# Row maxima of a softmax attention: negated in the reduction, transposed in 32x32 squares on VectorE, and brought to the query rows over DRAM instead of by a TensorE transpose

## The chip, the cores and the metric

The kernel runs on one core of a Trainium2 chip. The metric is the device time of one execution in microseconds; the median of three runs of the kernel before is 1742.61 us (1740.09 to 1744.63).

## The reference

One transformer block with adaptive layer norm, for 2048 rows of 512 numbers, all in float32:

```
mod = silu(c) @ w_mod                            # six rows of 512: sa, ca, ga, sb, cb, gb
h = layernorm(x) * (1 + ca) + sa
q, k, v = split(h @ wqkv)                        # 32 heads of 16
p = softmax(q @ k.T / 4)                         # 2048 x 2048 per head
x = x + ga * ((p @ v) @ wo)
h = layernorm(x) * (1 + cb) + sb
x = x + gb * (mish(h @ w1 + b1) @ w2)            # 1792 hidden columns
```

The softmax is a stable one: the largest score of each query row is taken off before the exponential. This document is about the way of these maxima.

## The kernel before, in words

Every float32 product is made of rounded pieces: a number is split into a high part (type float32r) and the low rest, and three products (high by high, high by low, low by high) are added in PSUM.

**Attention.** The work is cut into 32 groups of four heads by one block of 512 queries (`NIT`; group n = 8 * block + heads). A group has 16 steps. In a step of group n TensorE makes four score products of that group (`score`, L505: 128 keys by 512 queries, each with a contraction of 64 rows), four products of a later group for its maxima (`max_tile`, L468: 128 queries by 512 keys), eight products of probabilities by values for the step two before (`pv`, L523), and up to eight half products of other work (L130, through `mm_half`): projections of q, k and v for later blocks, then the output projection and the feed-forward part of an earlier block. ScalarE turns each score bank into probabilities (L508). VectorE reduces each bank of L468 to one column of maxima (L470, tile `mx`).

**The maxima, before.** The maxima run `PRO` = 20 steps ahead of the scores: those of group n are complete at the end of step 16n - 5. `neg_max` (L474) then makes the maximum over the four key blocks, twice, into the two halves of `mm` (L479). `max_rows` (L483) is called at the end of the next step through the table `ats`: TensorE transposes `mm` into a bank of the ring (L485), so that 128 queries by 32 columns become 32 rows; VectorE writes `mh` = -max rounded to float32r (L487), and `mt` (L488), which holds on the high rows -max rounded and on the low rows the rest, by a column `lows` of zeros and minus ones that is made at the start (L75 to L78). Four DMAs then write `mt` into rows 48 and 49 (and 112 and 113) of the query tiles `qa` of the group's two pairs of heads (L494). The key tiles hold ones in these rows, so the score product itself takes the maximum off. The first scores of the group read them in step 16n, four steps after `max_rows`.

**What sets the order.** Everything is written out by one loop over steps (`step`, L1091). A step has two half steps, and work that isn't a product is put in a table `hooks` by half step with `at` (L183): loads, puts and short VectorE work. Engines run their own instructions in that order and wait on semaphores. All DMAs are issued by SyncE, in the order of the hooks, on one queue; a DMA whose data or place isn't ready holds SyncE and all DMAs behind it. Others that the text speaks of: `load_q` and `load_k` (L291, L300) bring query and key rows from DRAM; `qk_unit`'s `put` (L250, L254) writes projected queries and keys to DRAM from the tiles `qh` and `ql`, which ScalarE fills from PSUM (L240); `prep_unit` (L645 to L657) splits weights and puts them to DRAM (`w1scr`, `woscr`, `w2scr`), in groups 1 to 7; `load_split` (L662) brings them back for the feed-forward part from group 8 on; `evac` (L531 on) sends the row sums as `rc` to DRAM (L559) and reads them back spread over rows (`rb`, L561).

**PSUM.** Six banks form a ring (`ring`, L145) for L468, L505, the transpose of L485 and some short products; two more (`ms`, `acc`) take the other work and the sums of L523.

Of the kernel before, what the change touches and what calls it, by code (L numbers as in the profile page):

```python
# [8 lines left out]
F32 = mybir.dt.float32  # L9
F32R = mybir.dt.float32r  # L10
AF = mybir.ActivationFunctionType
ALU = mybir.AluOpType
AX = mybir.AxisListType
# [5 lines left out]
def adaln_block(ctx: ExitStack, tc: tile.TileContext, x, wqkv, wo, w1, b1, w2, c, w_mod, out):  # L19
    nc = tc.nc  # L20
    P = 128
# [6 lines left out]
    TB = 512  # L28
# [3 lines left out]
    NIT = NB * G  # L32
# [6 lines left out]
    PRO = 16 + LEAD  # L39
# [7 lines left out]
    out = out[0]  # L47
# [3 lines left out]
    cst = ctx.enter_context(tc.tile_pool(name="cst", bufs=1))  # L51
    dram = ctx.enter_context(tc.tile_pool(name="dram", bufs=1, space=DRAM))
# [6 lines left out]
    w1scr = dram.tile([FT, P, 2, D], F32, name="w1scr")  # L59
    w2scr = dram.tile([FT, P, 2, D], F32, name="w2scr")  # L60
    rscr = dram.tile([NIT, 4, TB], F32, name="rscr")

    ident = cst.tile([P, P], F32, name="ident")
    make_identity(nc, ident)
# [7 lines left out]
    nc.gpsimd.memset(sel, 0.0)  # L72
    for k in range(DK):
        nc.gpsimd.memset(sel[32 * k:32 * k + 1, :], 1.0)
    lows = cst.tile([P, 1], F32, name="lows")  # L75
    nc.vector.tensor_reduce(out=lows[:32], in_=ident[:32, :32].rearrange("p (a v q) -> p v a q", a=4, v=2)[:, 1], op=ALU.add,
                            axis=AX.XY)
    nc.vector.tensor_scalar_mul(lows[:32], lows[:32], -1.0)  # L78
    modc = cst.tile([P, 4, DK], F32, name="modc")
    sil = cst.tile([P, DK], F32, name="sil")  # L80
    b1c = cst.tile([P, FT], F32, name="b1c")
# [2 lines left out]
    def dap(t, off, ap):  # L84
        return bass.AP(tensor=t.tensor, offset=t.offset + off, ap=ap)
# [59 lines left out]
    def ring(w=1):  # L145
        if w == 2 and ring_at[0] % 2:
            ring_at[0] += 1
        b = ring_at[0] % NRING
        ring_at[0] += w
        return ring_t[:, b, :] if w == 1 else ring_t[:, b:b + 2, :]  # L150
# [32 lines left out]
    def at(h, f):  # L183

        hooks.setdefault(h, []).append(f)


    NR = 5
    kq = ctx.enter_context(tc.tile_pool(name="kq", bufs=1))
    ka = [kq.tile([P, S], F32R, name=f"ka{i}") for i in range(2)]  # L190
    qa = [kq.tile([P, TB], F32R, name=f"qa{i}") for i in range(NR)]
# [257 lines left out]
    ap = ctx.enter_context(tc.tile_pool(name="ap", bufs=1, reuse_waits="tile"))  # L449
# [24 lines left out]
    def neg_max(n):  # L474

        mx = mxs.pop(n)
        mm = ap.tile([P, 4, 2, 4], F32, tag="mm", name="mm", bufs=2)
        for v in range(2):
            nc.vector.tensor_reduce(out=mm[:, :, v, :], in_=mx.rearrange("p s (j q) k -> p (s j) q k", j=2), op=ALU.max,  # L479
                                    axis=AX.X)  # L480
        ats.setdefault(16 * n + 16 - PRO, []).append(lambda: max_rows(n, mm))

    def max_rows(n, mm):  # L483
        pt = ring()
        nc.tensor.transpose(pt[:32, :P], mm.rearrange("p a v q -> p (a v q)"), ident)  # L485
        mh, mt = [ap.tile([32, P], F32R, tag=t, name=t, bufs=1) for t in ("mh", "mt")]
        nc.vector.tensor_scalar_mul(mh, pt[:32, :P], -1.0)  # L487
        nc.vector.scalar_tensor_tensor(mt, mh.bitcast(F32), lows[:32], pt[:32, :P], op0=ALU.mult, op1=ALU.subtract)  # L488

        def put():  # L490
            for j in range(2):
                for s in range(2):
                    o = (2 * s + j) * 8
                    nc.sync.dma_start(  # L494
                        qa[(2 * n + j) % NR][64 * s + 48:64 * s + 50, :].rearrange("v (s q) -> v s q", s=4).bitcast(F32),
                        mt[o:o + 8, :].bitcast(F32))
        at(2 * (16 * n + 16 - PRO) + 3, put)

    pts = {}

# [541 lines left out]
    ats = {}  # L1042
# [48 lines left out]
    def step(t):  # L1091
# [4 lines left out]
        if t < 0:  # L1096

            for i in range(2):
                if tm < 16:
                    kb, jq = divmod(2 * tm + i, 8)  # L1100
                else:
                    jq, kb = tm % 16 // 2, 2 * second + i
                for s in range(2):
                    max_tile(tm // 16, jq // 4, s, jq % 4, kb)()
            if second and tm % 16 == 15:
                neg_max(tm // 16)
            run_hooks(2 * t + 1)
            for f in ats.pop(t, []):
                f()
            whole_units(2 * t + 1, CREDIT)  # L1110
            do_specials(2 * t + 1)
            return
# [53 lines left out]
        if tm < T and tm % 16 == 15:  # L1166
            neg_max(tm // 16)
# [121 lines left out]
    t = T + 2  # L1289
# [32 lines left out]
```

## Time and profile before

| | |
|---|---|
| median of three runs | 1742.61 us (1740.09 to 1744.63) |
| the profiled execution | 1738.89 us, span 1737.1 us |
| TensorE busy | 1702.3 us (98%), 12396 instructions |
| VectorE busy | 1464.9 us (84%), 2464 |
| ScalarE busy | 1349.4 us (78%), 2581 |
| GpSimd busy | 729.0 us (42%), 723 |
| SyncE's DMA queue | 237.92 MB, its packets 48.0% of 16 DMA engines' span |
| mean granted TensorE clock | 0.998 |

How to read the profile: the page gives shares of the span for each engine (PE = TensorE matmuls, PEld = its weight loads, DVE = VectorE, ACT = ScalarE, POOL = GpSimd, SP = SyncE), the chain of work that ended last, and groups of instructions by line of the kernel. A row of a timeline is: start in us from the span's start, duration in us, engine, line, operation, written tile <- read tiles, shapes, count of merged instructions, and in brackets the idle time of the engine just before it with what ended that wait. "SPq" are SyncE's issues of DMAs: their duration is that of the issue and not of the transfer. A row of a group is: line, engine, operation, tiles, shapes, count | busy us in total, mean ns of one | idle us before them and what ended it. A row of the waits is: who waited <- for whom: us in total, times, longest us. The durations of matmuls are modelled and overlap, so distances between starts tell more than they do.

### The profile page before, as it was taken

Reading aid. Unit: us, or ns where it says so; the run is one execution under the profiler, and the core shown is the slowest. Engines: PE = TensorE matmul, PEld = TensorE weight load, DVE = VectorE, ACT = ScalarE, POOL = GpSimd, SP = SyncE. Lnnn points to the kernel's source line nnn. Section 1 sums busy time; section 2 is a strip of 40 time slices with the busy share of each in tenths; the row PEclk is TensorE's granted clock in tenths of the full one; section 3 lists DMA queues with packets and bytes.
Section 4 is the critical chain, followed back from the end, with each engine's and each line's share of the span. In section 5 each row is a group of like instructions: output and inputs, shape, how many; then the busy total and the mean of one; then the engine's idle time right before and its main releaser. Section 6 shows DMA issues by size and latency. Waiting matters only on the chain.

```text
span 1737.1 us, 33698 instructions
## 1 busy us (share of the span) xinstructions
PE 1702.3 (98%) x12396; PEld 963.9 (55%) x12396; DVE 1464.9 (84%) x2464; ACT 1349.4 (78%) x2581; POOL 729.0 (42%) x723
## 2 busy tenths in 40 slices
PE   7999999999999999999999999999999999999999
PEld 5755655555435555555555555555555555554587
DVE  6987888888898998989889898888898999892377
ACT  6257777777777898888877898888878988888474
POOL 5131124665303373444523374434423464444552
PEclk9999999999999999999999999999999999999999
DMA  7777467777762432524353533434252543423261
GB/s 251 187 254 189 114 172 202 234 235 223 218 184 52 136 96 77 136 77 121 89 137 87 162 97 88 139 90 124 71 156 73 152 102 103 115 79 130 85 230 61
DMA packets 113997, 240.08 MB, mean 138 GB/s; under 512 B 24048, under 2 KB 49648, under 8 KB 107784
## 3 DMA queue, kind: packets, MB, share of 16 engines
q1 hardware_dynamic: 113832, 237.92, 48.0%
q8 instruction: 98, 1.61, 0.4%
q14 instruction: 67, 0.55, 0.1%
HBM read 179.95 MB, written 51.44 MB: 133 GB/s over the span
## 4 chain that ended last, share of the span: by engine, by line
PE 80%; DMA 8%; DVE 4%; POOL 2%; ACT 2%; issue 2%; SPq 1%; POOLq 0%; ACTq 0%; DVEq 0%
PE bk L523 26%; PE ring L468 19%; PE ring L505 18%; PE bk L130 12%; PE ring L124 2%; DMA qscr<-ql 2%; DVE mx L470 2%; PE ring L1028 1%; DMA w1scr<-hl 1%; ACT pr L508 1%; PE bk L124 1%; DMA woscr<-hl 1%; DMA xt<-in_A_x 1%; DMA kscr<-ql 1%; DMA hl<-in_B_w 1%
## 5 line engine op out<-in xcount | busy, mean ns | idle before, releaser
L470 DVE TENSOR_REDUCE mx<-ring 128x1 f32<-128x512 f32 x2048 | 1274.0, 682 | 166.5 <-PE ring L468 134.7
L508 ACT ACTIVATE pr<-ring 128x512 f32<-128x512 f32 x2048 | 1083.3, 603 | 256.1 <-PE bk L130 161.4
L468 PE MATMUL ring<-ka,qa 64*128 64x512 f32 x2048 | 850.6, 429 | 0.9 <-DVE mx L470 0.4
L505 PE MATMUL ring<-qa,ka 64*128 64x512 f32 x2048 | 726.1, 398 | 7.0 <-ACT pr L508 5.8
L468 PEld LDWEIGHTS ring<-ka,qa 64*128 64x128 f32 x2048 | 366.4, 184 | 414.2 <-DVE mx L470 334.5
L523 PE MATMUL bk<-pr,vg 128*32 128x512 f32 x4096 | 546.3, 606 | 0.0
L505 PEld LDWEIGHTS ring<-qa,ka 64*128 64x128 f32 x2048 | 374.1, 185 | 88.3 <-ACT pr L508 34.4
L130 PE MATMUL bk<-h,w 64*128 64x512 f32 (+1 forms) x1080 | 279.0, 392 | 1.4 <-ACT pr L508 1.3
L130 PE MATMUL bk<-w,a_h 64*128 64x512 f32 x608 | 204.9, 416 | 1.4 <-ACT pr L508 1.2
L130 PEld LDWEIGHTS bk<-h,w 64*128 64x128 f32 x1080 | 178.5, 184 | 19.0 <-ACT pr L508 8.7
L723 POOL TENSOR_TENSOR hb<-hb,ee 128x512 f32<-128x512 f32 x42 | 54.0, 1286 | 293.9 <-DVE ee L722 293.9
L523 PEld LDWEIGHTS bk<-pr,vg 128*32 128x32 f32 x4096 | 81.6, 108 | 131.8 <-issue 126.0
L130 PE MATMUL bk<-w,a_l 64*128 64x512 f32 x304 | 119.4, 393 | 0.0
L130 PEld LDWEIGHTS bk<-w,a_h 64*128 64x128 f32 x608 | 100.9, 184 | 10.4 <-ACT pr L508 5.8
L865 POOL TENSOR_TENSOR y<-yd,y 128x512 f32<-128x512 f32 x48 | 62.0, 1295 | 80.4 <-ACT yd L864 80.2
L736 POOL TENSOR_TENSOR qq<-ee,rr 128x512 f32<-128x512 f32 x42 | 54.3, 1292 | 76.9 <-ACT rr L729 76.7
L130 PE MATMUL bk<-w,o_hl 64*128 64x512 f32 x288 | 81.5, 414 | 2.2 <-POOL o_hl L93 1.1
L96 POOL TENSOR_TENSOR a_l<-hb,a_h 128x512 fp32r<-128x512 f32 x53 | 72.3, 1363 | 4.4
L130 PEld LDWEIGHTS bk<-w,a_l 64*128 64x128 f32 x304 | 56.0, 184 | 3.0
L130 PE MATMUL bk<-h_h,wl 64*128 64x512 f32 x168 | 56.8, 419 | 0.0
L722 DVE SCALAR_TENSOR_TENSOR ee<-ee 128x512 f32<-128x512 f32 x56 | 41.4, 740 | 17.0 <-ACT ee L719 17.0
L738 POOL TENSOR_TENSOR rr<-rr,qq 128x512 f32<-128x512 f32 x42 | 54.1, 1287 | 3.5
(185 smaller groups left out, 1703.1 us busy)
## 6 DMA issues: line engine op xcount, KB each, us to landing
ka<-kscr SPq DMA_DIRECT2D x124, 384.0 KB
w<-w2scr SPq DMA_DIRECT2D x56, 512.0 KB
w<-w1scr SPq DMA_DIRECT2D x46, 512.0 KB
vg<-vscr SPq DMA_DIRECT2D x32, 552.0 KB
qa<-qscr SPq DMA_DIRECT2D x124, 100.0 KB
kscr<-qh SPq DMA_DIRECT2D x16, 512.0 KB
qscr<-qh SPq DMA_DIRECT2D x32, 256.0 KB
hl<-in_B_w SPq DMA_DIRECT2D x28, 256.0 KB
```

What stands on the lines that cost most here:

```text
L96: (nc.gpsimd if eng == "p" else nc.vector).tensor_sub(lo, src, hi.bitcast(F32))
L124: nc.tensor.matmul(acc, l, r, start=start, stop=stop)
L130: i = nc.tensor.matmul(acc, l[64 * g:64 * g + 64], r[64 * g:64 * g + 64], start=start and not g, stop=bool(stop and g))
L468: nc.tensor.matmul(pm, qt[64 * s:64 * s + 64, qs * P:(qs + 1) * P], kt[64 * s:64 * s + 64, kb * TB:(kb + 1) * TB], start=True, stop=True)
L470: nc.vector.tensor_reduce(out=mxs[n][:, s, 4 * j + qs, kb:kb + 1], in_=pm, op=ALU.max, axis=AX.X)
L505: nc.tensor.matmul(p_, kt[64 * s:64 * s + 64, kc * P:(kc + 1) * P], qt[64 * s:64 * s + 64, :], start=True, stop=True)
L508: e = nc.scalar.activation(pr, p_, AF.Exp, scale=SCALE)
L523: nc.tensor.matmul(accs[n][32 * h:32 * h + 32, :], vgs[n][:, o:o + 32], pts.pop((t, h)), start=(kc == 0), stop=(kc == 15))
L723: (nc.vector if tail else nc.gpsimd).tensor_mul(hb, hb, ee)
L736: nc.gpsimd.tensor_mul(qq, ee, rr)
L738: nc.gpsimd.tensor_mul(rr, rr, qq)
L865: nc.gpsimd.tensor_add(y[i], yd, y[i])
```

## The change

The transpose on TensorE goes, and with it its bank and the column `lows`. VectorE reduces with the sign turned round, twice: once into a float32r tile (the high part, `mh`), once into a float32 tile (`mm`). Their difference is the low part, written beside the high part by a subtraction in the first half of the next step (`split`, half step h). In that step's second half VectorE transposes the 128 x 32 tile in squares of 32 x 32 (`put`, h + 1): each square of 32 queries by 32 columns turns in place, so that `mt` holds, in its 32 rows of each quarter of the partitions, 32 of the 128 queries of a tile. One DMA writes the four squares side by side into a scratch `mscr` in DRAM (32 rows of 128). Three half steps later (`take`, h + 4) four DMAs read from there, each two rows of 512 numbers, into the query rows. Before, the four DMAs stood at h + 3 and read `mt` itself.

```diff
+    mscr = dram.tile([NIT, 32, P], F32, name="mscr")
...
-    lows = cst.tile([P, 1], F32, name="lows")
-    nc.vector.tensor_reduce(out=lows[:32], in_=ident[:32, :32].rearrange("p (a v q) -> p v a q", a=4, v=2)[:, 1], op=ALU.add,
-                            axis=AX.XY)
-    nc.vector.tensor_scalar_mul(lows[:32], lows[:32], -1.0)
...
     def neg_max(n):
 
         mx = mxs.pop(n)
-        mm = ap.tile([P, 4, 2, 4], F32, tag="mm", name="mm", bufs=2)
-        for v in range(2):
-            nc.vector.tensor_reduce(out=mm[:, :, v, :], in_=mx.rearrange("p s (j q) k -> p (s j) q k", j=2), op=ALU.max,
-                                    axis=AX.X)
-        ats.setdefault(16 * n + 16 - PRO, []).append(lambda: max_rows(n, mm))
-
-    def max_rows(n, mm):
-        pt = ring()
-        nc.tensor.transpose(pt[:32, :P], mm.rearrange("p a v q -> p (a v q)"), ident)
-        mh, mt = [ap.tile([32, P], F32R, tag=t, name=t, bufs=1) for t in ("mh", "mt")]
-        nc.vector.tensor_scalar_mul(mh, pt[:32, :P], -1.0)
-        nc.vector.scalar_tensor_tensor(mt, mh.bitcast(F32), lows[:32], pt[:32, :P], op0=ALU.mult, op1=ALU.subtract)
+        mm = ap.tile([P, 4, 4], F32, tag="mm", name="mm", bufs=2)
+        mh = ap.tile([P, 4, 2, 4], F32R, tag="mh", name="mh", bufs=1)
+        mt = ap.tile([P, 32], F32, tag="mt", name="mt", bufs=2)
+        hi = mh[:, :, 0, :]
+        for v in (hi, mm):
+            nc.vector.tensor_reduce(out=v, in_=mx.rearrange("p s (j q) k -> p (s j) q k", j=2), op=ALU.max, axis=AX.X,
+                                    negate=True)
+        h = 2 * (16 * n + 16 - PRO)
+
+        def split():
+            nc.vector.tensor_sub(mh[:, :, 1, :], mm, hi.bitcast(F32))
 
         def put():
+            nc.vector.transpose(mt, mh.rearrange("p a v q -> p (a v q)").bitcast(F32))
+            nc.sync.dma_start(dap(mscr, n * 32 * P, [[32, 4], [P, 32], [1, 32]]), mt)
+
+        def take():
             for j in range(2):
                 for s in range(2):
-                    o = (2 * s + j) * 8
-                    nc.sync.dma_start(
-                        qa[(2 * n + j) % NR][64 * s + 48:64 * s + 50, :].rearrange("v (s q) -> v s q", s=4).bitcast(F32),
-                        mt[o:o + 8, :].bitcast(F32))
-        at(2 * (16 * n + 16 - PRO) + 3, put)
+                    nc.sync.dma_start(qa[(2 * n + j) % NR][64 * s + 48:64 * s + 50, :].bitcast(F32),
+                                      dap(mscr, n * 32 * P + (2 * s + j) * 8 * P, [[TB, 2], [1, TB]]))
+        at(h, split)
+        at(h + 1, put)
+        at(h + 4, take)
```

## The prediction

> **What bounds the kernel now.** I read the page first: shares, chain of waits, groups. The execution that it shows took 1738.89 us; its span is 1737.1 us, so 1.8 us lie outside.
>
> ```profile
> span 1737.1 us, 33698 instructions
> PE 80%; DMA 8%; DVE 4%; POOL 2%; ACT 2%; issue 2%; SPq 1%; POOLq 0%; ACTq 0%; DVEq 0%
> ```
>
> Four fifths of the chain are TensorE. The second view is the timeline of one ordinary stretch, around the max_rows of group 21 (a group is four heads of one block of 512 queries; there are 32, and one takes some 47 us).
>
> ```profile
> 1097.09 1.07 PE L523 MATMUL bk<-pr,vg 128*32 128x512 f32 x8
> 1098.08 0.49 PE L468 MATMUL ring<-ka,qa 64*128 64x512 f32 x1
> ...
> 1098.23 0.34 DVE L479 TENSOR_REDUCE mm<-mx 128x16 f32<-128x64 f32 x2
> ...
> 1099.92 1.06 PE L523 MATMUL bk<-pr,vg 128*32 128x512 f32 x8
> ...
> 1100.92 0.28 PE L485 MATMUL ring<-ident,mm 128*32 128x128 f32 x1
> ...
> 1101.13 0.50 PE L468 MATMUL ring<-ka,qa 64*128 64x512 f32 x1
> ...
> 1101.92 2.82 SPq L494 DMA_DIRECT2D qa<-mt  x4
> ...
> 1103.04 1.06 PE L523 MATMUL bk<-pr,vg 128*32 128x512 f32 x8
> ...
> 1110.38 0.39 PE L505 MATMUL ring<-qa,ka 64*128 64x512 f32 x1
> ```
>
> The eight products of L523 close a step. From their start to the next product it takes 1098.08 - 1097.09 = 0.99 us in a plain step, and 1101.13 - 1099.92 = 1.21 us where the transpose of L485 stands between. The whole step takes 1099.92 - 1097.09 = 2.83 us against 1103.04 - 1099.92 = 3.12 us. TensorE is back to back in both, so the transpose costs 0.22 us of the path, less than its own 0.28 us. The row of 1110.38 is the first score of that group, the first reader of the maxima: it comes 1110.38 - 1101.13 = 9.2 us after the transpose's slot.
>
> The third view is where the path touches the DMAs: the first scores of groups 5, 6 and 7, in the timeline.
>
> ```profile
> 338.81 1.51 SPq L656 DMA_DIRECT2D woscr<-hl  x1
> 340.42 4.43 SPq L494 DMA_DIRECT2D qa<-mt  x4
> 344.94 0.74 SPq L291 DMA_DIRECT2D qa<-qscr  x2
> ...
> 346.55 0.50 PE L505 MATMUL ring<-qa,ka 64*128 64x512 f32 x1 [0.37 <-DMA qa<-mt]
> ```
>
> ```profile
> 395.14 0.49 PE L505 MATMUL ring<-qa,ka 64*128 64x512 f32 x1 [0.17 <-DMA qa<-mt]
> ```
>
> ```profile
> 443.98 0.50 PE L505 MATMUL ring<-qa,ka 64*128 64x512 f32 x1 [0.37 <-DMA qa<-mt]
> ```
>
> In these three groups the maxima are already the last thing that TensorE waits for. SyncE issued them from 340.42 on, and they released TensorE at about 346.5: some 6 us, because the query and weight transfers issued before are still in the queue. Nor is that the end of the queue's hold on the path:
>
> ```profile
> 359.23 0.58 ACT L240 COPY ql<-bk 128x512 f32<-128x512 f32 x1 [1.57 <-DMA qscr<-ql]
> ```
>
> ```profile
> 407.57 0.58 ACT L240 COPY ql<-bk 128x512 f32<-128x512 f32 x1 [1.70 <-DMA qscr<-ql]
> ```
>
> ```profile
> 456.26 0.58 ACT L240 COPY ql<-bk 128x512 f32<-128x512 f32 x1 [1.54 <-DMA qscr<-ql]
> ```
>
> Twelve microseconds after each, ScalarE waits for a put of queries (L250) that SyncE issues behind the maxima, and its copy empties the bank that TensorE wants. So from group 5 to group 7 what delays SyncE's queue delays TensorE.
>
> **The change part by part.** *The transposes on TensorE go.* 32 of them, 0.22 us each where TensorE is the bound. In groups 5 to 8 the DMA decides (below), and group 0's lies in the opening: 27 x 0.22 = 5.9 us gained; at the outside 32 x 0.22 = 7.0. The Trainium skill, VectorE: DVE Perf Modes, section "The three transpose paths", gives 390 ns for a 128x128 bf16 transpose on TensorE. By that figure 27 of them would be worth 10.5 us, an estimate, and the sum below would be +0.9 instead of +5.5. The rows above show 0.22 us for these f32 ones, and they decide. What is late next on TensorE is the next product, which has its operands; its ring bank is freed by VectorE.
>
> *VectorE.* The groups of its instructions:
>
> ```profile
> L470 DVE TENSOR_REDUCE mx<-ring 128x1 f32<-128x512 f32 x2048 | 1274.0, 682 | 166.5 <-PE ring L468 134.7 <-PE bk L130 29.3 <-PE ring L505 1.1
> L479 DVE TENSOR_REDUCE mm<-mx 128x16 f32<-128x64 f32 x64 | 11.1, 215 | 1.1
> L488 DVE SCALAR_TENSOR_TENSOR mt<-mh,lows,ring 32x128 fp32r<-32x128 f32 x32 | 10.7, 335 | 1.1
> L487 DVE TENSOR_SCALAR mh<-ring 32x128 fp32r<-32x128 f32 x32 | 8.9, 278 | 7.8 <-PE ring L485 6.2
> L558 DVE RECIPROCAL rc<-sm 128x16 f32<-128x16 f32 x31 | 7.5, 243 | 0.0
> L340 DVE TENSOR_TENSOR sil<-cc,sil_e 128x4 f32<-128x4 f32 x1 | 0.2, 161 | 0.0
> L78 DVE TENSOR_SCALAR lows<-lows 32x1 f32<-32x1 f32 x1 | 0.1, 141 | 0.0
> ```
>
> Before, a group costs 2 x 215 + 278 + 335 = 1043 ns. After: two reductions with the sign (430, the same shapes), a subtraction of 128x16 (161 to 243, from L340 and L558), a transpose of 128x32 in squares (between 141, L78, and 335, L488; I take 200). That is 732 to 1008 ns, 0.04 to 0.31 us less. I count nothing: TensorE's products hide it (VectorE idles 166.5 us before its 2048 reductions). Without that cover it would be worth up to 32 x 0.31 = 10 us in a gain, nothing in a loss. The two instructions of lows at the start go too: 0.3 us, ahead of a wait for ScalarE; nothing.
>
> *The way to the query rows.* Before, four DMAs per group go from mt to qa as soon as mt stands. After, one DMA writes mt to DRAM (the put), and four read it back (the takes); the first take waits on SyncE until the put has landed, with everything issued behind it. The put (16 KB in 128 pieces) follows the sign and two more reductions, in the step before the old transpose: in group 21 the L479 end at 1098.57, then 0.2 + 2 x 0.68 + 0.2 us, so 1100.3, where the first DMA left at 1101.9. In SyncE's order put and takes stand next to each other in 20 groups; in groups 0, 1, 2, 8, 17, 18, 21, 23, 25, 26, 29 and 31 one to four other transfers lie between, which now queue behind the put's wait for VectorE. The trace has this path once already: the reciprocals of the row sums go to DRAM (L559) and come back (L561) with the same wait. An idle and a loaded place, in the timeline of SyncE:
>
> ```profile
> 1130.76 0.34 SPq L559 DMA_DIRECT2D rscr<-rc  x1
> 1132.19 0.60 SPq L561 DMA_DIRECT2D rb<-rscr  x1
> ```
>
> ```profile
> 466.44 0.34 SPq L559 DMA_DIRECT2D rscr<-rc  x1
> 466.89 0.37 SPq L662 DMA_DIRECT2D w<-woscr  x1
> 472.93 0.61 SPq L561 DMA_DIRECT2D rb<-rscr  x1
> ```
>
> 1.4 us and 6.5 us. For a take's landing, the nearest row is the first load of the kernel, 2 KB on an idle queue, issued at 0.72 and ending ScalarE's wait at 2.93, so 2.2 us:
>
> ```profile
> 0.72 0.44 SPq L310 DMA_DIRECT2D cc<-in_c  x1
> ...
> 2.93 0.21 ACT L337 ACTIVATE sil_e<-cc 128x4 f32<-128x4 f32 x1 [0.93 <-DMA cc<-in_c]
> ```
>
> *Late groups (9 to 31), with the queue idle:* in group 21 the put goes out at 1100.3, the takes at 1101.7 and then every 0.33 to 0.61 us (0.37 per L291, 0.61 per L561), the last landing by 1101.7 + 3 x 0.61 + 2.2 = 1105.7. The first score stands at 1110.4. More than 4 us to spare, so nothing lost. What SyncE has behind the takes is issued no later than now, since it follows four issues now too. What lies between put and takes is later: in group 21 the last of four weight loads,
>
> ```profile
> 1087.03 4.41 SPq L662 DMA_DIRECT2D w<-w2scr  x4
> ...
> 1115.93 0.47 PE L130 MATMUL bk<-w,a_h 64*128 64x512 f32 x1
> ```
>
> which moves from 1091.1 to about 1100.9 behind the put. The next product that reads such weights starts at 1115.93: 15 us for a load, so it is hidden.
>
> *Groups 5 to 7, the loaded queue.* SyncE cannot reach the put before 340.4, since woscr<-hl (338.81) stands ahead of it in both orders. The put lands about when the maxima land now, 346.5: 6.1 us, against 6.5 for the row of 466.44. Only then do the takes go. The first score, of the pair's odd head, needs the second of them: 0.33 to 0.61 later and 2.2 us to land, so 349.0 to 349.3 in place of 346.55: **2.5 to 2.8 us**. The transfers that SyncE issues behind (qa<-qscr at 344.94 now) go out after four take issues, at 347.9 to 349.0, and the queue has run dry: it stands empty for 1.3 to 2.4 us of issues and about 2.2 us until bytes come, 3.5 to 4.6 us, of which some 0.6 belongs to the next transfer anyway. The put of queries that ScalarE waits for at 359.23 is then 2.9 to 4.0 us late, and TensorE's wait there grows to that. The same three rows stand in groups 6 and 7, so I take 3.4 us each: 10.2 us, between 3 x 2.5 = 7.5 and 3 x 4.0 = 12.0.
>
> *Group 8* has a full queue and two steps of its own:
>
> ```profile
> 483.39 2.87 SPq L494 DMA_DIRECT2D qa<-mt  x4
> ...
> 490.91 0.50 PE L505 MATMUL ring<-qa,ka 64*128 64x512 f32 x1
> ```
>
> The put goes at about 482, the four weight loads follow it, the takes leave at about 482 + 6.5 = 488.5 and land behind the loads, the second one by 488.5 + 0.6 + 2.2 = 491.3 or up to 1.5 us later: 0.4 to 1.9 us, I take 1.0. *Group 0*: the opening has three puts and a weight slice in the queue beside it; 0 to 1 us, I take 0.3. *Groups 1 to 4:* SyncE stands ready there, so even a put of 6.5 us brings the second take 6.5 + 0.6 + 2.2 = 9.3 us after its issue, and the first score comes 1110.4 - 1100.3 = 10.1 us after it; nothing, with 0.8 us in hand.
>
> **Sum:** -5.9 + 10.2 + 1.0 + 0.3 = +5.6 us; 1738.9 + 5.6 = 1744.5 against the profiled execution. That one is 3.7 us below the median of the runs shown (1742.61), so I carry the difference over: 1742.6 + 5.6 = **1748.2 us**. Its own range: from -7.0 + 7.5 + 0.4 = +0.9 to -5.4 + 12.0 + 1.9 + 1.0 = +9.5, so 1743.5 to 1752.
>
> **The rivals.** *A: the put does not wait for the queue, and the change is faster.* What decides is when the put of groups 5 to 7 lands: if by 346.5 - 2.8 = 343.7, the second take is there at 346.5, no step loses anything, and all that remains is the transposes: -7.0 us, 1735.6. For it: a narrow transfer can overtake a wide one.
>
> ```profile
> SPq L300 <- DMA woscr<-hl: 0.8, 1, 0.8
> ```
>
> This row of SyncE's waits between 338 and 350 us: it was held until 346.9 by woscr<-hl, issued at 338.81, when the maxima issued after it had released TensorE. The Trainium skill, DMA: Bandwidth & Descriptors, section "Queues, rings and completion order", says that completion is not in order of issue, since each DMA engine has a ring of its own; the trace agrees by that 0.4 us. By that rule a put on few engines could be the early one. Against it: the overtaking is 0.4 us, not 2.8, and the row of 466.44 waited 6.5 us. Chance 0.13.
>
> *B: the 0.22 us do not come back,* since VectorE sets the step there (its work of the two reductions, subtraction and transpose now falls into one step, 0.8 us beside 4 x 0.68 in 2.83). Then the losses stand alone: +11.5 us, 1754. Against it: the old L487 and L488 put 0.61 us into one such step, and that step took only the 0.22 us more. Chance 0.10.
>
> *C: the late groups lose too,* if a round trip there takes 4 us more than 1.4 + 2.2: from that point on each of 23 groups pays. One extra microsecond is 23 us, 1771. Against it: 1130.76 to 1132.19 is a late place, at 1.4 us. Chance 0.05.
>
> *D: the dry queue costs nothing beyond itself,* because the steps of groups 5 to 7 have other waits in which it vanishes (ScalarE's of 1.5 us): 3 x 1.5 = 4.5 us less, +1.1, 1743.7, no change that can be told. Chance 0.15.
>
> **How the numbers follow.** About 0.3%, 5.2 us, is what a measurement of this kernel tells from no change: below 1737.4 is faster, above 1747.8 slower. My forecast has 0.57; its own range (1743.5 to 1752) lies half below 1747.8: 0.25 the same, 0.32 slower. With A to faster, D to the same, B and C to slower: 0.13, 0.40, 0.47. The range of 8 in 10 must take in B and part of A: 1736 to 1756 leaves out C and the far half of A.
>
> **What would show it.** The interval from L523 to the next L468 beside the old transposes is 0.99 us instead of 1.21 in the late groups. At the first scores of groups 5, 6 and 7 TensorE's wait names DMA qa<-mscr and has grown from 0.2 to 0.4 us to about 3; SyncE's waits show a new row, the take for mscr<-mt, some 6 us in these groups and about 1.4 in the late ones. Late groups show no wait for qa<-mscr. I am wrong if the waits in groups 5 to 7 stay under 1 us each (A), or if late steps take 3.1 us still (B).

## The result, and the profile after

The kernel after takes 1753.48 us (median of five runs, 1750.91 to 1759.25), the kernel before 1740.72 us beside it (median of five): a ratio of **1.0076, interval [1.0062, 1.0091]**, 13 us slower. The forecast was 5.6 us slower, in a range of 1736 to 1756. The execution that the page shows took 1759.25 us with a span of 1757.5 us, the longest of the five and 5.8 us above their median. Below, a difference in us against the kernel before is (ratio - 1) x 1740.

From the page after, the span and the head of the chain of work:

```profile
span 1757.5 us, 33667 instructions
...
PE 78%; DVE 7%; DMA 7%; ACT 3%; POOL 2%; issue 1%; SPq 1%; POOLq 0%; DVEq 0%; ACTq 0%
```

VectorE holds 7% of the chain instead of 4%: the first sign that something happened where the forecast counted nothing. The groups of VectorE in the kernel after:

```profile
L467 DVE TENSOR_REDUCE mx<-ring 128x1 f32<-128x512 f32 x2048 | 1276.3, 683 | 190.5 <-PE ring L465 155.6 <-PE bk L127 32.5 <-PE ring L505 1.6
L484 DVE TENSOR_TENSOR mh<-mm,mh 128x16 fp32r<-128x16 f32 x32 | 12.5, 391 | 1.1
...
L479 DVE TENSOR_REDUCE mh<-mx 128x16 fp32r<-128x64 f32 x32 | 7.0, 220 | 1.1
L479 DVE TENSOR_REDUCE mm<-mx 128x16 f32<-128x64 f32 x32 | 6.7, 209 | 0.0
L487 DVE STREAM_TRANSPOSE mt<-mh 128x32 f32<-128x32 f32 x32 | 6.3, 198 | 0.0
```

The reductions (209 to 220 ns) and the transpose (198) are as forecast. The subtraction, L484, is not: 391 ns in the mean, where 161 to 243 were taken. The view of its tile shows why a mean says little here (minimum, median, maximum in ns):

```profile
L484 DVE TENSOR_TENSOR mh<-mm,mh x32: 174/176/1237, 94.0 to 1586.0; 128x16 fp32r<-128x16 f32 x32
```

Of the 32, 19 take 174 to 178 ns and 13 take 472 to 1237. Each of these 13 starts while a GpSimd instruction runs and ends 17 to 35 ns after it. The timeline around the maxima of group 22 shows one of them:

```profile
1159.39 1.06 PE L523 MATMUL bk<-pr,vg 128*32 128x512 f32 x8
...
1160.98 0.22 DVE L479 TENSOR_REDUCE mh<-mx 128x16 fp32r<-128x64 f32 x1
1161.11 0.21 DVE L479 TENSOR_REDUCE mm<-mx 128x16 f32<-128x64 f32 x1
...
1161.20 0.63 POOL L735 TENSOR_SCALAR ee<-ee 128x512 f32<-128x512 f32 x1
1161.36 0.48 DVE L484 TENSOR_TENSOR mh<-mm,mh 128x16 fp32r<-128x16 f32 x1
...
1162.50 0.50 PE L505 MATMUL ring<-qa,ka 64*128 64x512 f32 x1 [0.45 <-DVE mx L467]
...
1163.00 1.07 PE L523 MATMUL bk<-pr,vg 128*32 128x512 f32 x8
...
1163.19 0.60 SPq L488 DMA_DIRECT2D mscr<-mt  x1
...
1164.00 0.49 PE L465 MATMUL ring<-ka,qa 64*128 64x512 f32 x1
...
1165.20 1.16 SPq L493 DMA_DIRECT2D qa<-mscr  x4
...
1165.85 1.06 PE L523 MATMUL bk<-pr,vg 128*32 128x512 f32 x8
```

The same steps in the kernel before:

```profile
1143.96 1.06 PE L523 MATMUL bk<-pr,vg 128*32 128x512 f32 x8
...
1147.05 1.07 PE L523 MATMUL bk<-pr,vg 128*32 128x512 f32 x8
...
1150.10 1.07 PE L523 MATMUL bk<-pr,vg 128*32 128x512 f32 x8
```

Read the first of the two from the bottom. From L523 to the next product it takes 1164.00 - 1163.00 = 1.00 us, where it took 1.21 in group 21 of the kernel before: the transpose's 0.22 us are there. The step with the transpose now takes 1165.85 - 1163.00 = 2.85 us (before, in this group, 3.05). But the step ahead of it takes 1163.00 - 1159.39 = 3.61 us (before 3.09). In it the subtraction starts at 1161.36 and ends at 1161.84; a GpSimd instruction that started at 1161.20 ends at 1161.83. The reductions of L467 behind it are late, and TensorE waits 0.45 us for a bank. More is lost than the transpose gave.

In the loaded groups, the first scores of groups 5 and 6, SyncE's timeline and, in the last line, its waits between 330 and 354 us:

```profile
349.30 0.50 PE L127 MATMUL bk<-h_h,wh 64*128 64x512 f32 x1 [1.32 <-ACT ql L237]
...
352.75 0.79 PE L505 MATMUL ring<-qa,ka 64*128 64x512 f32 x1 [2.94 <-DMA qa<-mscr]
```

```profile
404.20 0.50 PE L505 MATMUL ring<-qa,ka 64*128 64x512 f32 x1 [1.50 <-DMA qa<-mscr]
```

```profile
344.31 1.54 SPq L488 DMA_DIRECT2D mscr<-mt  x1
350.91 1.21 SPq L493 DMA_DIRECT2D qa<-mscr  x4
```

```profile
SPq L493 <- DMA mscr<-mt: 5.0, 1, 5.0
```

SyncE waits 5.0 us for the put to land (some 6 were forecast), and TensorE 2.94 us for the takes (about 3 were). Another wait of 1.32 us, for ScalarE, stands just ahead. What the forecast did not have is the duration of the product at 352.75: 0.79 us instead of 0.50. The windows view of the same stretch (length, busy us and counts of PE, PEld, DVE, ACT, POOL, then the granted clock, DMA share and GB/s):

```profile
346.50:350.40 3.90, 1.98 (x11) 0.51 (x10) 1.80 (x3) 1.58 (x3) 2.06 (x2) 1.00 0.44 165
350.40:357.20 6.80, 4.45 (x20) 2.03 (x20) 2.08 (x3) 2.28 (x4) 3.91 (x5) 0.50 0.51 117
357.20:362.00 4.80, 4.80 (x39) 2.81 (x35) 3.68 (x6) 3.65 (x8) 0.41 (x1) 1.00 0.99 274
```

After a stretch in which TensorE was half idle, its clock is granted at 0.50 for 6.8 us. The Trainium skill, TensorE: Matmul & The Clock Gate, section "Part 1: The HAM clock gate", says that the array's clock is halved after an idle window of some 3.4 us. The trace agrees in the length of the pieces, 3.4 and 6.8 us; but TensorE was not idle for a whole window here, it was busy for 1.98 of 3.90 us. The traces of all thirteen kernels show what it takes here. Within an execution every halving starts on a grid of 3.41 us. Between 120 and 1700 us there are 42 halvings, and in the grid's window ahead of each TensorE was busy for 17 to 58% of the time; of the 5936 windows at full clock that no halving followed, all but five were busy for more than that.

To see where time went, I took the starts of the first product of L523 in each step and compared the way between them with the profiled execution of before, in three stretches. "Loaded" runs from the third step of group 4 to that of group 9, which holds the first scores of groups 5 to 9, and "late" from there to the end of group 31. "Halved" is the sum of the stretches with a clock of 0.50 between 60 and 1700 us.

| us against before | ratio of the times | loaded | late | halved |
|---|---|---|---|---|
| before | 1 | 0 | 0 | 6.8 |
| after | 1.0076 [1.0062, 1.0091] | +10.6 | +2.7 | 30.7 |
| e1: rest from one input, a third reduction | 1.0046 [1.0028, 1.0064] | +8.9 | -1.3 | 20.5 |
| e2: old way in groups 5 to 8 | 1.0016 [1.0005, 1.0027] | +2.7 | +2.2 | 10.2 |
| e3: e1 and e2 | 0.9996 [0.9984, 1.0008] | +0.4 | -0.8 | 6.8 |
| e4: before, with the DRAM trip alone | 1.0069 [1.0053, 1.0084] | +10.7 | -0.4 | 20.5 |
| e5: rest from one input, two reductions | 1.0029 [1.0018, 1.0041] | +7.6 | -2.9 | 17.1 |
| e6: e5 and e2 | 0.9982 [0.9971, 0.9992] | +1.3 | -2.7 | 10.2 |
| e7: puts of groups 5 to 8 by ScalarE | 1.0073 [1.0059, 1.0087] | +10.2 | +2.7 | 20.5 |
| e8: before, with a two-input subtraction | 1.0054 [1.0039, 1.0069] | +2.6 | +7.9 | 10.2 |
| e9: e6, rest one step later | 0.9966 [0.9954, 0.9978] | -2.7 | -3.7 | 3.4 |
| e10: before, with a one-input reduction | 1.0018 [1.0007, 1.0030] | +2.4 | +1.9 | 17.1 |
| e11: after, TensorE kept busy once | 1.0061 [1.0041, 1.0080] | +8.7 | +1.8 | 17.1 |

The stretches come from one execution of each kernel. What is missing to the spans lies in the opening and the tail: in the kernel after 3.3 and 3.8 us, the first ahead of its first put and so not the change's. The loaded stretch scatters: e6 and e9 do the same there and differ by 4 us. The execution shown of the kernel after is the longest of its five, with the lowest mean clock (0.990, the others 0.993 to 0.996), so its loaded stretch is a long one. Even so this stretch parts the kernels: the six with the trip over DRAM in groups 5 to 8 (after, e1, e4, e5, e7, e11) lie at +7.6 to +10.7, the seven without it at -2.7 to +2.7. The late stretch is steadier: four kernels that do the same there (after, e2, e7, e11) lie between 1.8 and 2.7.

### The profile page after: what moved, and what is told of

Read it like the earlier page. It is cut to its first block, busy times and chain, and to the rows that moved or that the text cites. A ratio compares the mean times of both kernels' runs of the same rounds, so it can differ in the third digit from the quotient of the medians.

```text
span 1757.5 us, 33667 instructions
## 1 busy us (share of the span) xinstructions
PE 1707.3 (97%) x12364; PEld 971.2 (55%) x12364; DVE 1462.8 (83%) x2462; ACT 1352.4 (77%) x2581; POOL 730.1 (42%) x723
## 4 chain that ended last, share of the span: by engine, by line
PE 78%; DVE 7%; DMA 7%; ACT 3%; POOL 2%; issue 1%; SPq 1%; POOLq 0%; DVEq 0%; ACTq 0%
PE bk L523 26%; PE ring L465 20%; PE ring L505 18%; PE bk L127 11%; DVE mx L467 3%; DMA qscr<-ql 2%; PE bk L121 1%; ACT pr L508 1%; DMA rb<-rscr 1%; PE ring L121 1%; DVE qq L731 1%; DVE ee L722 1%; DMA kscr<-ql 1%; DMA woscr<-hl 1%; ACT rr L726 1%
## 5 line engine op out<-in xcount | busy, mean ns | idle before, releaser
L467 DVE TENSOR_REDUCE mx<-ring 128x1 f32<-128x512 f32 x2048 | 1276.3, 683 | 190.5 <-PE ring L465 155.6
L523 PE MATMUL bk<-pr,vg 128*32 128x512 f32 x4096 | 547.4, 607 | 0.0
L523 PEld LDWEIGHTS bk<-pr,vg 128*32 128x32 f32 x4096 | 81.7, 108 | 133.2 <-issue 127.4
```

The lines of the kernel that those rows point to most:

```text
L467: nc.vector.tensor_reduce(out=mxs[n][:, s, 4 * j + qs, kb:kb + 1], in_=pm, op=ALU.max, axis=AX.X)
L523: nc.tensor.matmul(accs[n][32 * h:32 * h + 32, :], vgs[n][:, o:o + 32], pts.pop((t, h)), start=(kc == 0), stop=(kc == 15))
```

## The experiments

**Theory R** says that the round trip in the loaded queue costs; **theory S** that the subtraction with two inputs from SBUF is held by GpSimd; **rival B** that VectorE is simply full in that step.

**e1, one-input rest.** A third reduction writes the maxima, rounded and without the sign, beside the negated ones; a reduction by addition over the pairs replaces the subtraction.

```diff
-            nc.vector.tensor_sub(mh[:, :, 1, :], mm, hi.bitcast(F32))
+                nc.vector.tensor_reduce(out=mh[:, :, 1, :], in_=mp.bitcast(F32), op=ALU.add, axis=AX.X)
```

> The kernel after, with the subtraction made from one input: a third reduction writes the maxima without the sign, rounded, beside the exact negated ones, and a reduction by addition over these pairs gives the rest. 0.21 us of VectorE more per group, nothing else changed. The kernel after stands 12.8 us over the kernel before. Theory S (the two-input subtraction of L484 is held while a GpSimd instruction runs, up to 1.24 us, and the steps beside it lose some 0.8 us in about half of the late groups): the reduction takes about 0.2 us everywhere, the steps of 3.4 to 3.9 us beside it go back to about 2.85, and 7 to 8 us come back: 4.5 to 6 us over the kernel before. Rival B (VectorE is simply full in that step): 0.21 us more work there, so the time stays or grows: 12 to 16 us over the kernel before. Theory R (only the round trip over DRAM in groups 5 to 8 costs): no change, 12 to 13 us over.

8.0 us over before, between the theories: 5 us came back. The step of the reductions takes 3.18 us in the mean of groups 9 to 29 (before 2.99, after 3.35), while 0.21 us of VectorE were added. So S has a part in it; what B has, this run alone can't tell (e5, e10).

**e2, the old way in groups 5 to 8**, and **e3, both.**

```diff
+        if 5 <= n <= 8:
...
+            ats.setdefault(16 * n + 16 - PRO, []).append(lambda: max_rows(n, m4))
+            return
```

> The kernel after, with the old way (transpose on TensorE, four direct DMAs) in groups 5 to 8 only, the new way in the other 28. Theory R (the round trip in the loaded queue of groups 5 to 8 is what costs): the waits for the maxima at the first scores of groups 5 to 7 go back to 0.2 to 0.4 us, the halvings of the clock after them go, and 8 to 11 us come back: 2 to 5 us over the kernel before. Theory S (held subtraction): its share in groups 9 to 31, 7 to 8 us, stays, which is the same number as long as both hold, so what tells them apart is this run beside e1: their gains add up if both hold. If the round trip costs nothing, 12 to 13 us over the kernel before.

> e1 and e2 together: the old way in groups 5 to 8, the one-input rest in the other 28. If the round trip of groups 5 to 8 and the held subtraction are all that costs, what is left is the gain of 27 transposes at 0.22 us less some small things of the groups 0 and 9: 3 to 6 us under the kernel before. If either theory is wrong, it stays 4 us or more over it.

e2: 2.8 us over, 10 us came back; between the two profiled executions the loaded stretch gives back 7.9 us and the late one 0.5. So R holds, at the size expected. e3: 0.7 us under, less than the 3 to 6 expected: no theory of the two explains all, since the late groups gain only 0.8 us where 23 x 0.22 = 5.1 were to be had. The rest is B's, with the third reduction's 0.21 us per group in it (e5, e9, e10).

**e4, the trip alone.** The kernel before, whose four rows go over DRAM.

```diff
-        at(2 * (16 * n + 16 - PRO) + 3, put)
+        at(h + 2, put)
+        at(h + 4, take)
```

> The kernel before (transpose on TensorE, sign and rest on VectorE as it was), with only the way of the maxima changed: a put of the 32 rows to DRAM at half step h+2 and four takes at h+4 instead of the four direct DMAs at h+3. Theory R: the first scores of groups 5 to 7 wait some 3 us longer, groups 8 and 9 a little, late groups nothing: 8 to 12 us over the kernel before. If the late groups lose in the round trip as well (rival C): 20 us or more. If the trip costs nothing and the held subtraction is all: within 2 us of the kernel before.

12.0 us over, 10.7 of them in the loaded stretch, nothing in the late one. Its first score of group 5 has the same wait as the kernel after:

```profile
352.54 0.79 PE L509 MATMUL ring<-qa,ka 64*128 64x512 f32 x1 [2.71 <-DMA qa<-mscr]
```

and the trip of a late group, with an idle queue, takes 1.4 us from put to takes:

```profile
1162.26 0.32 SPq L492 DMA_DIRECT2D mscr<-mt  x1
1163.66 1.15 SPq L497 DMA_DIRECT2D qa<-mscr  x4
```

R is shown, and rival C is out: late groups do not pay for the trip.

**e5, the rest from one input without more instructions.** The high part keeps its sign, with minus ones in its row of the key tiles; the negated maxima lie in the same tile, and one reduction by addition gives the rest. **e6** is e5 with the old way in groups 5 to 8.

```diff
-                                    negate=True)
+                                    negate=v is mm)
...
+        nc.gpsimd.memset(one[:4, :], -1.0)
```

> The kernel after, with the rest made from one input and without a third reduction: the high part keeps its sign (the key tiles hold minus ones in its row), the exact negated maximum lies in the same tile, and one reduction by addition over the pairs gives the rest. VectorE has as many instructions as in the kernel after, and none with two inputs from SBUF. In the run with a third reduction 4.8 us came back (12.8 to 8.0 over the kernel before), while the step of the reductions still took 3.18 us against 2.99 in the kernel before. Theory S (the held subtraction is what ate the gain): that step goes to 2.95 to 3.05 and the late groups gain 0.15 to 0.2 us each, so 3 to 4 us more come back: 3.5 to 5.5 us over the kernel before, the rest being the round trip. Rival B (VectorE is full in that step whatever the form): the step stays at 3.15 or above, 7 to 9 us over.

> The kernel of the run before this with the old way (transpose on TensorE, direct DMAs) in groups 5 to 8. The one with a third reduction and the old way there stood 0.7 us under the kernel before. Theory S: 3 to 4 us less, so 3.5 to 5 us under the kernel before, faster than both kernels. Rival B: 0 to 1 us under.

5.0 us over, as S has it, and 3.1 us under, 0.4 short of S. The rest now has one duration, beside GpSimd or not:

```profile
L487 DVE TENSOR_REDUCE mh<-mh x32: 185/188/191, 94.5 to 1574.6; 128x16 fp32r<-128x32 f32 x32
```

The two steps around the maxima of group 22, as distances between the starts of L523 (L526 in e5):

```
                   step of the reductions   next step
before                      3.09              3.05
after                       3.61              2.85
e5                          3.29              2.84
mean of the steps that lie in groups 9 to 29:
before                      2.99              3.10
after                       3.35              2.91
e5                          3.08              2.93
e9                          3.02              2.93
```

In group 22 the 0.2 us that VectorE has more in the first step come out one for one. That is B at work, at 0.1 us in the mean.

**e7, the put on another queue.**

```diff
-            nc.sync.dma_start(dap(mscr, n * 32 * P, [[32, 4], [P, 32], [1, 32]]), mt)
+            (nc.scalar if 5 <= n <= 8 else nc.sync).dma_start(dap(mscr, n * 32 * P, [[32, 4], [P, 32], [1, 32]]), mt)
```

> The kernel after, with the put of groups 5 to 8 alone issued by ScalarE on its own queue, so that it stands behind no transfer of SyncE; the takes stay on SyncE. Theory Q (the put is late because it stands behind the transfers in SyncE's queue): it lands in 2 to 3 us, before SyncE comes to the takes, SyncE's wait for it (6 us) goes, the takes leave when the direct DMAs left before, and 8 to 10 us come back: 3 to 5 us over the kernel before. Rival E (it is late because the DMA engines are full, on whichever queue it stands): it still lands 5 to 6 us after its issue, and ScalarE loses some 0.5 us per put as well: 11 to 15 us over.

12.7 us over: no better. In group 5, ScalarE's issue and its next work, SyncE's takes, and SyncE's wait:

```profile
335.69 1.09 ACTq L488 DMA_DIRECT2D mscr<-mt  x1
336.82 1.58 ACT L508 ACTIVATE pr<-ring 128x512 f32<-128x512 f32 x3 [2.97 <-DVE mx L467]
```

```profile
343.39 1.21 SPq L493 DMA_DIRECT2D qa<-mscr  x4
```

```profile
SPq L493 <- DMA mscr<-mt: 4.2, 1, 4.2
```

The put is issued by 336.8 and lands at 343.4, 6.6 us later, on a queue on which nothing stands ahead of it. So rival E is right for the landing: the place in SyncE's queue is not what makes the trip long. The DMA engines were busy for 0.73 of these 6.6 us, and for 0.05 of the 1.4 us of e4's late trip; that this load is the reason is argued, not shown. The first score of that group no longer waits, as the put left early enough; but ScalarE stood 3 us for it, and its step took 5.43 us instead of 2.90 in the kernel after.

**e8, the subtraction in the kernel before**, and **e10, the control with one input.** Nothing reads either result.

```diff
+            nc.vector.tensor_sub(dm, mm[:, :, 0, :], mm[:, :, 1, :])
```

```diff
+            nc.vector.tensor_reduce(out=dm, in_=mm.rearrange("p a v q -> p a q v"), op=ALU.add, axis=AX.X)
```

> The kernel before, with one added instruction per group that nothing reads: a subtraction of 128x16 with both inputs in SBUF on VectorE, at the half step at which the kernel after has its own (16 steps by 32 groups are otherwise unchanged). Theory S: it takes 0.18 us where GpSimd is idle and up to 1.2 us where a GpSimd instruction runs, the steps beside it grow by 0.5 to 1 us in about half of the late groups: 4 to 8 us over the kernel before. If 0.18 us of VectorE more in a step are hidden and nothing holds the subtraction: within 1 us of the kernel before.

> The control to the subtraction added to the kernel before (9.4 us over it): in its place an instruction with one input, a reduction by addition of the same tile's pairs to 128x16, that nothing reads. Theory S: it takes 0.19 us everywhere, and what is left is VectorE's time alone: 1 to 3 us over the kernel before. If the place in the step or one more instruction is what costs, and not the second input: 7 to 10 us over, as with the subtraction.

9.4 us over, against 3.1. The tile's view of e8, then of e10:

```profile
L485 DVE TENSOR_TENSOR dm<-mm x32: 174/176/1282, 94.1 to 1580.6; 128x16 fp32r<-128x16 f32 x32
```

```profile
L485 DVE TENSOR_REDUCE dm<-mm x32: 186/187/192, 94.6 to 1574.7; 128x16 f32<-128x32 f32 x32
```

One instruction of 176 ns in an otherwise unchanged kernel costs 7.9 us in the late stretch, one of 187 ns in the same place 1.9. The difference, 6 us, is the second input. In e8 15 of the 32 take 472 to 1282 ns, and each ends 18 to 34 ns after a GpSimd instruction that was running when it began; in e10 17 begin beside a running one, and none is held: S shown. The 1.9 us are B.

**e9, the rest a step later** (groups 9 to 31; otherwise e6).

```diff
+        late = 2 if n >= 9 else 0
+        at(h + late, split)
+        at(h + late + 1, put)
+        at(h + late + 4, take)
```

> The kernel with the signs and the old way in groups 5 to 8 (3.1 us under the kernel before), with the rest, the transpose and the put of groups 9 to 31 one step later (half steps h+2 and h+3) and their takes at h+6. The two reductions then stand alone in their step, as in the kernel before. In that run the step of the reductions took 3.08 us and the next one 2.93 (means of groups 9 to 29), against 2.99 and 3.10 in the kernel before. Rival B as far as it was seen (VectorE sets that step in about half of the groups): the first goes to 2.99 or below, the second stays under 3.0, 1.5 to 2.5 us come back: 4.5 to 5.5 us under the kernel before. If the second step grows by what the first loses: 3 us under. If the later trip over DRAM comes too late for the first scores (2 us to spare by the trace): over the kernel before.

5.9 us under before, ratio 0.9966 [0.9954, 0.9978]: **faster than both kernels**. The late stretch gains 1.0 us on e6 (-3.7 against -2.7), half of what was expected and no more than that stretch scatters, though its step of the reductions does fall from 3.08 to 3.02 us. The rest of the gain on e6 lies in the loaded stretch, where the two do the same, so I do not count it to the edit.

**e11, the clock kept.** Eight products of the identity ahead of group 5's first score, in the kernel after (the trace lists each as two).

```diff
+            for _ in range(8 if (n, j, s, kc) == (5, 0, 1, 0) else 0):
+                nc.tensor.matmul(p_[:, :P], ident, ident, start=True, stop=True)
```

> The kernel after, with eight products of the identity with itself (128 columns, some 0.25 us each) into the bank of group 5's first score just ahead of it, so that TensorE has work for 2 us of the 2.9 us for which it waits there. Theory K (such a wait halves the granted clock for 3.4 to 6.8 us behind it, and that costs as much as the wait): the halving at 350 us goes, the step of that score and the next go from 9.1 and 3.7 us to some 6.4 and 2.9: 2 to 4 us less than the kernel after, 9 to 11 over the kernel before. If the halved clock costs nothing since the steps wait anyway: the same as the kernel after, 12 to 14 over.

The timeline and the windows:

```profile
346.45 2.05 PE L506 MATMUL ring<-ident 128*128 128x128 f32 x16
349.51 0.50 PE L507 MATMUL ring<-qa,ka 64*128 64x512 f32 x1 [1.01 <-DMA qa<-mscr]
```

```profile
343.00:350.00 7.00, 4.63 (x32) 2.68 (x30) 1.99 (x4) 1.76 (x4) 5.46 (x6) 1.00 0.40 141
350.00:357.00 7.00, 7.00 (x56) 3.94 (x52) 5.78 (x10) 5.98 (x12) 1.91 (x2) 1.00 0.88 198
```

The clock stays at 1.00, and the two steps take 7.99 + 2.89 us instead of 9.11 + 3.67: 1.9 us less in that place, though the maxima are no earlier. The time, 10.6 us over before, has an interval that overlaps that of the kernel after, so the gain of the whole is not shown. Another halving came at 365 us, where the kernel after had none, and the step there took 5.80 us against 3.96: three steps on, the 1.9 us were lost again.

## Why the prediction was right in direction and half in size

**The transposes.** Right: 0.19 us less per group in the step of the old transpose (3.10 to 2.91 in the mean). Over the 22 groups whose maxima fall in the late stretch that step gave 4.2 us and the step behind it 1.2, together 5.3 us unrounded, where 23 x 0.22 = 5.1 were to be had.

**VectorE: this is the step that failed.** It was counted at nothing, with "nothing in a loss" as its worse end. Measured, the subtraction with two inputs costs 7.9 us in the late stretch (e8), and -5.1 + 7.9 = +2.8 is what the kernel after shows there (+2.7). Its steps say the same: +7.5 us in the steps of the reductions, -5.3 in the two steps behind them, +0.5 in all others. The price of 161 to 243 ns came from L340, which ran once, and from L558, which has one input; neither had GpSimd beside it with both inputs in SBUF. The trace of before held the warning, in rows that the prediction did not use, line L96 on VectorE:

```profile
L96 DVE TENSOR_TENSOR h_l<-hf,h_h x5: 1026/1157/1529, 21.2 to 48.9; 128x512 fp32r<-128x512 f32 x5
L96 DVE TENSOR_TENSOR ql<-ring,qh x5: 678/682/691, 29.4 to 51.3; 128x512 fp32r<-128x512 f32 x5
...
L96 DVE TENSOR_TENSOR a_l<-hb,a_h x3: 691/692/693, 1718.7 to 1729.9; 128x512 fp32r<-128x512 f32 x3
```

One line, one shape: 682 ns with an input from PSUM (ring), 692 with both from SBUF in the tail, where no GpSimd instruction ran beside it, and 1026 to 1529 with both from SBUF in the opening, where one had begun ahead of each of the five. Nor did the old L487 and L488 have this: they read PSUM. The Trainium skill, SBUF — State Buffer, section "Who interferes with whom", states the rule: an instruction of VectorE with two SBUF inputs contends with a GpSimd instruction that reads SBUF, and the one that is issued first keeps the shared port for its whole length; a reduction never contends. The runs agree: every held subtraction ends within 35 ns of the end of a GpSimd instruction that began before it, and it is 174 to 1282 ns with two inputs against 185 to 192 with one. By this rule the kernel's 32 subtractions were a rival that the prediction lacked.

**The loaded groups.** The sum was 10.2 + 1.0 us. By the medians the trip in groups 5 to 8 costs 10.4 us (after against e2), 8.7 (e1 against e3) and 8.1 (e5 against e6). The size is nearly right, and the first half of the working too: the put's trip of 6.1 us (6.6, 6.1 and 6.2 us from its issue to the takes in groups 5 to 7), a wait of about 3 us at group 5's first score (2.94). But it was right partly by chance. The waits in groups 6 and 7 were smaller than forecast (1.50 us, and none for the takes in group 7), and group 8's 1.0 us did not come: its put took 3.5 us, and no wait for the takes followed. ScalarE's later wait was to grow to 2.9 to 4.0 us; in the three places it was

```profile
366.87 0.59 ACT L237 COPY ql<-bk 128x512 f32<-128x512 f32 x1 [0.98 <-DMA qscr<-ql]
```

```profile
418.02 0.59 ACT L237 COPY ql<-bk 128x512 f32<-128x512 f32 x1 [3.10 <-DMA qscr<-ql]
```

```profile
468.13 0.59 ACT L237 COPY ql<-bk 128x512 f32<-128x512 f32 x1 [1.96 <-DMA qscr<-ql]
```

against 1.57, 1.70 and 1.54: one of three as forecast. The loss that was measured has two parts, waits and the halved clock, which the prediction did not have at all. In the loaded stretch the waits that the profile lists for TensorE grew from 11.2 to 18.3 us, 7.1 of the 10.6 us; the other 3.5 us are products that took longer, in a stretch that had 20.5 us at a clock of 0.50 against 6.8 before. These are single executions, and how much of the loss the clock has in the medians is open; e11 shows 1.9 us for one halving of 6.8, lost again a little later.

Nor is the halving at group 5 the trip's alone. The clock also fell there, at 346.9 to 349.3 us, in e2, e3, e6, e8 and e10, which have no trip in group 5, behind waits of 1.6 to 2.2 us for ScalarE. Of the seven kernels without the trip only the kernel before (0.78 us for ScalarE there) and e9 (0.55) show no halving at that place, so what group 5 loses against the execution shown of before is not the price of the trip.

**The rivals.** A (the put overtakes) is out: it took 6.6 us, even from a queue of its own. B holds in part: VectorE sets the step in some groups, at 1.9 us in all for 0.19 us more per group (e10). B's time, 1754 us, is close to the measured 1753.5 by luck: it took the 0.22 us per group for lost, and they came back. C is out (e4). D's mechanism, a wait that vanishes in another, showed once, at 366.87, and was outweighed.

**The sum.** Late +2.7 instead of -5, loaded +10.6 against +11.2: 13.3 us, as the ratio has it (13.2). That they agree so closely is chance, since the two executions differ by 20.4 us, with the opening and the tail, and the loaded stretch scatters by 4. The forecast missed 13.2 - 5.6 = 7.6 us, and the held subtraction, at 7.9, is as large as that. The measured 1753.48 us lies above the prediction's own range of 1743.5 to 1752 and inside 1736 to 1756 only because that range was to take in B as well.

Two numbers of the working do not follow from its terms, and nothing hangs on them: with 27 transposes at 10.5 us the sum would be +1.0 instead of +5.6, not +0.9 instead of +5.5, and the -5.4 in the upper end of the range is worked out nowhere.

## What to carry to other kernels

Before an instruction is moved onto VectorE, look at where its inputs lie and at what GpSimd does beside it: a small operation with two inputs from SBUF that begins while GpSimd runs such an instruction as here lasts until that one ends, and a reduction with one input was held in no run. Price a new instruction by rows with the same kinds of operands, and read minimum and maximum, not the mean. A wait that leaves TensorE busy for less than about half of 3.4 us is to be priced with the halved clock behind it, and a DRAM round trip by a trip in the same place: 1.4 us with an idle queue, 6.1 to 6.6 us in groups 5 to 7. Before a stretch is read as the cost of a change, look at how much it differs between kernels that do the same there.

## What the runs showed of the hardware that was not expected

- A 128x16 subtraction on VectorE with both inputs in SBUF: 174 ns alone, up to 1282 ns beside GpSimd; a one-input reduction of the same output 185 to 192 ns throughout.
- A put of 16 KB took 6.6 us to land from a second, empty queue while the DMA engines were busy for 0.73 of the time, no less than from the loaded one.
- TensorE's clock fell to 0.50, for 3.4 or 6.8 us, behind 42 windows of 3.41 us in which TensorE was busy for 17 to 58%, and it stayed at 1.00 behind all windows with more; 2.05 us of products without use kept it at 1.00 at group 5 in one execution.
